# A windowed attention with Fourier mixing: batch 0's scalings on ScalarE, and the whole order of work planned anew

## The chip, the cores and the metric

The kernel runs on one core of a Trainium2 chip. Five engines of the core work side by side, each with its own queue of instructions in a fixed order: TensorE (PE in the profile; its weight loads are PEld), VectorE (DVE), ScalarE (ACT), GpSimd (POOL) and SyncE (SP), which here issues DMAs only. An instruction waits on semaphores for what it needs, and everything behind it in the same queue waits with it. The metric is the device time of one execution in microseconds (us), lower is better; the time of a version is the median of its runs.

## What is computed

Four batches of 8 heads, 768 positions and head size 64. Each position attends to the first 8 positions and to the last 96 ones, with a slope per head. The output x (768 x 512 per batch) goes through a two-dimensional Fourier transform of which the real part is kept, a normalization, and a two-layer network with 2048 hidden values.

```python
scores = scale * np.matmul(q, k.transpose(0, 1, 3, 2)) + bias      # (4, 8, 768, 768)
scores = np.where(is_global | is_local, scores, -1e9)
a = np.exp(scores - np.max(scores, axis=-1, keepdims=True))
attn = np.matmul(a / (np.sum(a, axis=-1, keepdims=True) + 1e-09), v)
x = attn.transpose(0, 2, 1, 3).reshape(B, S, H * D)                # (4, 768, 512)
mixed = np.real(np.fft.fft(np.fft.fft(x, axis=1), axis=2))
u = x + mixed
un = (u - mean(u)) / np.sqrt(var(u) + 1e-06)                       # over the last axis
out = u + np.maximum(un @ w_ch1, 0.0) @ w_ch2
```

## The kernel before

**Stages.** Batch b = 0..3 has four pairs of heads hp = 0..3. For each pair q, k and v are loaded on SP's queue (`load`, token `("ld", 4b+hp, which)`), cast to fp16 (`qk`, `vc`), transposed (`pt` on TensorE for batches 0 and 1, evicted as `qkT`; by DMA for batches 2 and 3), multiplied into scores (`sc`, three groups each), passed through the exponential on ScalarE (`ex`, or `er` and a product on VectorE for batches 2 and 3), and multiplied with v (`av`). `norm` (lines 778 to 785) divides and writes `x`, token `("x", b, hp, jp)` with jp = 0..2. v itself is placed by small matmuls (`pv`) and two evictions, `("v", b, hp, 0)` on VectorE and `("v", b, hp, 1)` on ScalarE.

**The transform.** `fold_s` (lines 813 to 856) adds and subtracts parts of x in four steps f1 to f4, `fold_d` gives the operands `w`, `y_unit` (`py`) and `u_unit` (`pu`) are the two matrix stages, with `mirror` reversing some of y on GpSimd. Batch 0's x is also written to DRAM and read back in another order (`bounce`, tokens `xw` and `xr`) on SP's queue, and batch 1's v loads stand behind that read in the same queue. `u` is the sum, `un` its normalized copy, `ptu` its transpose, `unT` the eviction of that.

**The network.** Each batch gives three chunks, c = 0..11, of 256 positions. `ph(c, j)`, j = 0..7, is one unit of the first layer: 8 matmuls of 256 columns, evicted as `h(c, j)`. `pg(c, t, p)` is a unit of the second layer: 4 matmuls of 512 columns, t = 0, 1, p = 0..3. `ph(c, j)` needs quarter j // 2 of the first weight matrix, w1(j // 2); `pg(c, t, p)` needs quarter p of the second, w2(p). The eight quarters are loaded by eight DMAs on GpSimd's queue (`wload`, lines 1440 to 1457), w1(0) to w2(3) in this order, into memory that first holds batch 1's q and k. The last four chunks use a product scheme with fewer multiplications (`pg_units`, banks `pgA` and `pgD`).

**What sets the order.** Nothing is written in the order in which it runs. Each piece of work is handed to a planner (`Plan`, from line 21) with what it needs, the engines that may do it with a duration for each, and a rank. The planner walks through a model of the engines' clocks and always emits what can start first; `LAND` holds arrival times of some loads, and `BIAS` (lines 142 to 145) adds some microseconds to the start time of single pieces in that comparison, so that they are emitted earlier or later. A PE unit can be chosen from the next 10 of the streams MIX and ATT, and from the head of PH and PG. So a changed duration or preference can move any instruction on any engine. The order that comes out is fixed in the program: what is emitted first on an engine runs first there, and the planner's times play no part on the chip.

**Banks.** Results of TensorE lie in PSUM banks in rings: `xx` has two, `ph` two, `pg` two; C and D exist for the first part only, and the `ph` and `pg` banks take their place, so that the first `ph` unit waits for the last reader of C and D. The planner gives each unit one bank of its ring, and the unit then waits until that bank's eviction is done.

Of the kernel before, what the change touches and what calls it, by code (L numbers as in the profile page):

```python
# [9 lines left out]
FP16 = mybir.dt.float16  # L10
FP32 = mybir.dt.float32
AF = mybir.ActivationFunctionType
ALU = mybir.AluOpType

P = 128
# [7 lines left out]
class Plan:  # L23
# [110 lines left out]
    def slot(self, tag):  # L134
# [4 lines left out]
        return tag  # L139

    LOOK = 10
    BIAS = {(1, 92): -0.3, (3, 34): 0.7, ('h', 7, 7): -3, (2, 58): 3, (3, 69): -1.5, (1, 22): -0.3, ('mk1', 1): -3, (1, 26): -0.7, (2, 46): 0.7,
            ('ex', 0, 1, 1): 0.3, ('h', 2, 0): 1.5, ('h', 2, 6): -0.7, (1, 5): -1.5, ('er', 2): -0.7, (2, 32): -0.7, (3, 45): -1.5, ('er', 0): -0.7,
            (2, 50): -0.7, ('w2t', 0): -1.5, ('ss', 0, 1): -0.7, (3, 66): -1.5, ('unT', 7): 1.5, ('x', 3, 0, 1): -3, ('xb', 14, 0): 0.3,
            (1, 93): -1.5, (2, 35): -3, (3, 22): 0.3, ('ld', 11, 2): 0.7, (2, 36): 0.3, ('y', 1, 2, 3, 'r'): 0.7}
    AHEAD = 0.0

    def run(self, streams):
# [40 lines left out]
def act(n):  # L189
    return 0.06 + n / 1200.0  # L190


def dve(n):
    return 0.085 + n / 960.0


def dve2(n):
    return 0.075 + n / 1920.0
# [7 lines left out]
def kernel(  # L206
# [84 lines left out]
    pl = Plan()  # L291
# [23 lines left out]
    def free(tag, i):  # L315
        i -= NBUF[tag]
        return [("free", tag, i)] if i >= 0 else []

    def buf(tag, i, shape, dtype, users):
        pl.users(("free", tag, i), users)  # L320
        return wk.tile(shape, dtype, tag=f"{tag}_{i % NBUF[tag]}", name=f"{tag}_{i}", bufs=1)
# [186 lines left out]
    def CD(b, ring):  # L508
        if b == 1 and ring in ("C", "D"):
            pl.left[("CD",)][0] += 1  # L510
            return [("CD",)]
        return [("CD",)] if b == 0 else []
# [224 lines left out]
    def av(b, part, jp):  # L737

        half, nh = part[0] // 2, 2 * len(part)
        first = 2 * part[0]  # L740
        needs = [("ex", b, hp, g) for hp in part for g in range(max(jp - 1, 0), jp + 1)]
        needs += VN(b, part)
        if jp:
            needs += [("eg", b, half), ("vG", b, half)]

        def run(start, ring):
            po = bank(ring, f"pav_{b}_{first}_{jp}")
            n = 0
            for jj in range(2):
                j = 2 * jp + jj  # L750
                if jp:
                    nc.tensor.matmul(po[:, jj, 0:65 * nh].rearrange("p (h d) -> p h d", d=65),  # L752
                                     EG[:, (j - 2) * P:(j - 1) * P], vG[b % 2][:, first:first + nh, 0:65],
                                     start=True, stop=False, skip_group_check=True)
                for hh in range(nh):
                    h = first + hh
                    hp, s = h // 2, h % 2
                    ops = [(expst[hp][:, s, j * 256:j * 256 + P], j)]
                    if j:
                        c0 = (j - 1) * 256 + P  # L760
                        ops.append((expst[hp][:, s, c0:c0 + P], j - 1))
                    for a, (lhsT, i) in enumerate(ops):
                        nc.tensor.matmul(po[:, jj, hh * 65:(hh + 1) * 65], lhsT, v16[b % 2][:, i, h, 0:65],  # L763
                                         start=(jp == 0 and a == 0), stop=(a == len(ops) - 1),
                                         skip_group_check=True)
                        n += 1
            e = pl.pe(mm_us(65, n) + (mm_us(65 * nh, 2) if jp else 0), start)
            if jp:
                for _ in part:
                    pl.used(("free", "eg", b), e)  # L770
            if jp == NP - 1:
                for hp in part:
                    pl.tok[("avh", b, hp)] = e
                if part[-1] == HP - 1:
                    pl.tok[("avdone", b)] = e
            pv = po[:, :, 0:65 * nh].rearrange("p j (h d) -> p j h d", d=65)

            def norm():
                if b not in X:
                    X[b] = buf(XT[b][0], XT[b][1], [P, NS, Dm], FP16, 4)  # L780
                rc = wk.tile([P, 2, nh, 1], FP32, tag="rc", name=f"rc_{b}_{first}_{jp}", bufs=2)
                V.reciprocal(rc, pv[:, :, :, 64:65])
                VT(X[b][:, 2 * jp:2 * jp + 2, first * Dh:(first + nh) * Dh].rearrange("p j (h d) -> p j h d", d=Dh),  # L783
                   pv[:, :, :, 0:Dh], rc.to_broadcast([P, 2, nh, Dh]), op=ALU.mult)
            pl.later([("DVE", 0.09 + dve(128 * nh), norm)], free(*XT[b]), e, [("x", b, hp, jp) for hp in part], CD(b, ring),
                     ring=ring, rank=RA(b))
        ATT.append((needs, BANKS(b), run))


    T = {}  # L790
# [22 lines left out]
    def fold_s(b):  # L813
# [3 lines left out]
        for n, (c0, cw) in enumerate(parts):  # L817
# [10 lines left out]
                VT(ab[:, 1], lo, hi, op=ALU.subtract)  # L828

            def f2(c0=c0, cw=cw, n=n, cell=cell):  # L830
                pm = cell["pm"] = buf("ww", IW(b, n), [P, 2, 2, cw], FP16, 1)
                ab = cell["ab"]
                VT(pm[:, 0], ab[:, :, 1], ab[:, :, 2], op=ALU.add)
                VT(pm[:, 1], ab[:, :, 1], ab[:, :, 2], op=ALU.subtract)

            def f3(c0=c0, cw=cw, cell=cell):
                ab, pm, zc = cell["ab"], cell["pm"], T[("z", b)][:, :, c0:c0 + cw]
                VT(zc[:, 0], ab[:, 0, 0], pm[:, 0, 0], op=ALU.add)
                VT(zc[:, 1], ab[:, 1, 0], pm[:, 1, 1], op=ALU.subtract)
                V.tensor_scalar_mul(zc[:, 4], pm[:, 1, 0], c)  # L840
                V.tensor_scalar_mul(zc[:, 5], pm[:, 0, 1], c)

            def f4(c0=c0, cw=cw, cell=cell):
                ab, pm, zc = cell["ab"], cell["pm"], T[("z", b)][:, :, c0:c0 + cw]
                V.scalar_tensor_tensor(zc[:, 2], pm[:, 0, 0], -0.5, ab[:, 0, 0], op0=ALU.mult, op1=ALU.add)
                V.scalar_tensor_tensor(zc[:, 3], pm[:, 1, 1], 0.5, ab[:, 1, 0], op0=ALU.mult, op1=ALU.add)
            last = n == len(parts) - 1
            pl.later([("DVE", 2 * dve2(3 * cw), f1)],
                     [("x", b, hp, jp) for hp in hps for jp in range(NP)] + free("eA", IA(b, n))
                     + (free("zy", 2 * b) if n == 0 else []), 0.0,  # L850
                     [("f1", b, n)], [("free",) + XT[b]] * (2 if len(hps) == HP else 1))
            pl.later([("DVE", 2 * dve2(2 * cw), f2)], [("f1", b, n)] + free("ww", IW(b, n)), 0.0, [("f2", b, n)])
            pl.later([("DVE", 4 * dve2(cw), f3)], [("f2", b, n)], 0.0, [("f3", b, n)])
            pl.later([("DVE", 2 * dve(cw), f4)], [("f3", b, n)], 0.0, [("z", b, n)],
                     [("free", "eA", IA(b, n)), ("free", "ww", IW(b, n))])
        return [("z", b, n) for n in range(len(parts))]

    def IA(b, n):

# [5 lines left out]
    def IW(b, n):  # L865

        return n if b == 0 else 1 + 3 * b + n
# [165 lines left out]
    def u_unit(b, pr):  # L1033
# [4 lines left out]
        def run(start, ring):  # L1038
# [56 lines left out]
                else:  # L1095
                    V.tensor_scalar(cell[0][:, a], UT[c][:, a], SC, m, op0=ALU.mult, op1=ALU.add)  # L1096
            for a in range(2):
                pl.later([("ACT", 0.52, lambda a=a: un("ACT", a)), ("DVE", 0.38, lambda a=a: un("DVE", a))],
                         [("u", c, a)] + free("un", c), 0.0, [("un", c, a)])

            def square(a):
# [473 lines left out]
```

## Time and profile before

| | |
|---|---|
| median of 8 runs | 266.44 us (264.51 to 267.31) |
| the profiled execution | 265.24 us, of which the span of the profile is 263.3 us |
| PE busy | 247.3 us, 94% of the span, 2648 matmuls |
| PEld busy | 181.0 us, 69% |
| DVE busy | 178.6 us, 68%, 366 instructions |
| ACT busy | 140.3 us, 53%, 238 instructions |
| POOL busy | 70.4 us, 27%, 138 instructions |
| mean granted clock | 0.992 |

The span is what the profile shows from the first to the last instruction; 1.94 us of the profiled execution lie around it. Times in the profile are counted from the start of the span. Matmuls are pipelined, so a busy PE can still be waiting for the next operand: a unit's cost is read from the distance between the starts of successive units (a `ph` unit in a full stretch takes 0.87 us, a `pg` unit 0.86 us), not from the busy time. Instructions whose queue entry waits are listed with the idle time in front of them and with what ended it.

### The profile page before, as it was taken

How to read it: one execution, taken by the hardware profiler on the slowest of the kernel's cores; microseconds unless marked ns; L12 is line 12 of the kernel's file. 1: busy time of each engine (PE TensorE's matmuls, PEld its weight loads, DVE VectorE, ACT ScalarE, POOL GpSimd, SP SyncE). 2: the span in 40 equal slices, each digit the busy share in tenths (PEclk: the TensorE clock that was granted, in tenths of full speed). 3: DMA queues.
4: the chain of work that ended last, by engine and by line, in shares of the span. 5: the costliest groups of instructions: out<-in, count | busy, mean ns of one | idle time of the engine just before them, and what ended most of it. 6: DMA issues, size and time to landing. Idle time of an engine off the chain costs nothing.

```text
span 263.3 us, 6439 instructions
## 1 busy us (share of the span) xinstructions
PE 247.3 (94%) x2648; PEld 181.0 (69%) x2648; DVE 178.6 (68%) x366; ACT 140.3 (53%) x238; POOL 70.4 (27%) x138
## 2 busy tenths in 40 slices
PE   8788778899999999899999999999999999999994
PEld 2566456578765786676665565687578968888883
DVE  4458999964389756672579958669997665616173
ACT  1378597777416556793561464993044464353410
POOL 1435358951041145323320352103000411010000
PEclk9799999999999999999999999999999999999999
DMA  7999959999499955965898996403163230402022
GB/s 216 292 293 302 312 141 270 216 212 206 102 211 289 331 126 147 202 166 125 219 172 187 265 219 130 92 12 73 41 159 122 74 88 0 122 0 80 2 80 80
DMA packets 76381, 41.95 MB, mean 159 GB/s; under 512 B 33474, under 2 KB 72514, under 8 KB 76354
## 3 DMA queue, kind: packets, MB, share of 16 engines
q1 hardware_dynamic: 69298, 32.65, 52.2%
q0 software_dynamic: 4224, 4.19, 9.5%
q10 hardware_dynamic: 2832, 4.72, 6.0%
q8 instruction: 20, 0.33, 0.5%
q14 instruction: 7, 0.06, 0.1%
HBM read 31.59 MB, written 9.44 MB: 156 GB/s over the span
## 4 chain that ended last, share of the span: by engine, by line
PE 72%; DVE 15%; ACT 5%; DMA 3%; issue 2%; SPq 1%; POOL 0%; DVEq 0%; ACTq 0%
PE ph L1161 28%; PE pg L1185 20%; PE pgD L1266 5%; PE pav L763 4%; PE pgA L1266 4%; PE py L964 3%; PE pu L1044 3%; ACT er L649 2%; DMA u<-in_v_dram 2%; DVE qkT L581 2%; PE sc L625 2%; PE pav L752 1%; DVE u L1072 1%; DVE un L1096 1%; DVE x L783 1%
## 5 line engine op out<-in xcount | busy, mean ns | idle before, releaser
L1161 PE MATMUL ph<-unT,w 128*128 128x256 f16 x768 | 92.8, 273 | 0.3 <-DVE u L1072 0.3
L1161 PEld LDWEIGHTS <-w 128*128 128x128 f16 x768 | 73.2, 98 | 13.3 <-issue 2.5
L1167 ACT ACTIVATE hT<-ph 128x512 f16<-128x512 f32 x77 | 45.8, 597 | 61.5 <-PE ph L1161 61.4
L1185 PE MATMUL pg<-w,hT 128*128 128x512 f16 x256 | 59.5, 380 | 0.0
L1185 PEld LDWEIGHTS <-hT 128*128 128x128 f16 x256 | 24.1, 98 | 25.0 <-issue 0.6
L649 ACT ACTIVATE er<-sc 128x992 f16<-128x992 f32 (+2 forms) x24 | 21.4, 930 | 7.2 <-PE sc L625 5.4
L652 ACT ACTIVATE ex<-sc 128x992 f16<-128x992 f32 (+2 forms) x24 | 20.7, 931 | 3.4 <-PE sc L628 3.4
L664 DVE TENSOR_TENSOR ex<-er,mk 128x992 f16<-128x992 f16 (+2 forms) x24 | 16.0, 683 | 4.8 <-ACT er L649 4.8
L1012 POOL COPY ww<-zy 128x512 f16<-128x512 f16 x16 | 9.7, 627 | 34.6 <-PE py L964 34.6
L1194 DVE SCALAR_TENSOR_TENSOR u<-pg,sm,u 128x512 f32<-128x512 f32 x16 | 11.9, 746 | 8.9 <-PE pg L1185 8.9
L1168 DVE TENSOR_SCALAR hT<-ph 128x512 f16<-128x512 f32 x19 | 13.1, 687 | 6.9 <-PE ph L1161 6.8
L410 POOL CAST qk<-qs 128x768 f16<-128x768 f32 x12 | 10.1, 848 | 27.3 <-DMA qkT<-qk 13.8
L1110 POOL TENSOR_SCALAR sm<-sm 128x2 f32<-128x2 f32 x12 | 2.5, 211 | 54.3 <-ACT un L1103 52.7
L763 PEld LDWEIGHTS <-ex 128*128 128x128 f16 x352 | 15.1, 97 | 2.8 <-issue 2.1
L763 PE MATMUL pav<-v,ex 128*128 128x65 f16 x352 | 16.4, 193 | 0.2 <-ACT v L486 0.2
L1103 ACT ACTIVATE un<-un 128x512 f16<-128x512 f16 x24 | 15.0, 625 | 0.6 <-PE ptu L1133 0.6
L1063 DVE SCALAR_TENSOR_TENSOR u<-pu,xr 128x512 f32<-128x512 f32 x18 | 11.7, 687 | 5.2 <-PE pu L1044 5.2
L1284 DVE SCALAR_TENSOR_TENSOR u<-pgD,sm,u 128x512 f32<-128x512 f32 (+1 forms) x9 | 6.2, 691 | 11.2 <-PE pgD L1266 11.0
L1266 PEld LDWEIGHTS <-hT 128*128 128x128 f16 x128 | 12.5, 98 | 1.8 <-issue 0.4
L783 DVE TENSOR_TENSOR x<-pav,rc 128x512 f16<-128x512 f32 (+1 forms) x21 | 12.9, 615 | 0.7
L539 POOL COPY kG<-qkT 64x8 f16<-64x8 f16 x32 | 7.8, 245 | 16.7 <-DVE qkT L581 13.6
L496 POOL CAST v<-qs 128x768 f16<-128x768 f32 x8 | 7.4, 923 | 18.2 <-DMA qs<-in_v_dram 18.2
(122 smaller groups left out, 386.6 us busy)
## 6 DMA issues: line engine op xcount, KB each, us to landing
out_dram<-u SPq DMA_DIRECT2D x23, 256.0 KB, 2.2
w<-in_moe_w_ch_dram POOLq DMA_DIRECT2D x8, 512.0 KB, 19.2
qs<-in_q_dram SPq DMA_DIRECT2D x9, 384.0 KB, 3.9
qs<-in_k_dram SPq DMA_DIRECT2D x9, 384.0 KB, 5.4
qs<-in_v_dram SPq DMA_DIRECT2D x16, 192.0 KB, 4.5
xr<-xd ACTq DMA_DIRECT2D x3, 768.0 KB, 5.0
u<-in_v_dram SPq DMA_DIRECT2D x5, 384.0 KB, 7.4
w<-in_q_dram SPq DMA_DIRECT2D x4, 384.0 KB, 6.3
```

Source lines behind the costliest of these rows:

```text
L649: A(mine(), cut(pa), AF.Exp, 0.0, 0.125)
L652: A(cut(expst[hp][:, :, g * 512:g * 512 + (384 if g == 2 else 512)]), cut(pa), AF.Exp, 0.0, 0.125)
L664: VT(o, mine(), m, op=ALU.mult)
L763: nc.tensor.matmul(po[:, jj, hh * 65:(hh + 1) * 65], lhsT, v16[b % 2][:, i, h, 0:65], start=(jp == 0 and a == 0), stop=(a == len(ops) - 1) ...
L783: VT(X[b][:, 2 * jp:2 * jp + 2, first * Dh:(first + nh) * Dh].rearrange("p j (h d) -> p j h d", d=Dh), pv[:, :, :, 0:Dh], rc.to_broadcast( ...
L1103: A(x, x, AF.Square, accum_out=MV[c][:, a, 2:3])
L1161: nc.tensor.matmul(ph[:, a * CH:(a + 1) * CH].rearrange("p (x m) -> p x m", x=2), W1[0][:, d, jb * P:(jb + 1) * P], UNT[c][:, :, d, :], st ...
L1167: pl.later([("ACT", act(512), lambda: A(dst, ph, AF.Relu)), ("DVE", dve(512), lambda: V.tensor_scalar_max(dst, ph, 0.0))], [], e, [("h", c ...
L1168: ("DVE", dve(512), lambda: V.tensor_scalar_max(dst, ph, 0.0))],
L1185: nc.tensor.matmul(pg, HT[c][:, jb, t * P:(t + 1) * P], W2[0][:, jb, :], start=(jb == 0), stop=(jb == NJ - 1))
L1194: V.scalar_tensor_tensor(UT[c][:, t, :], pg, MV[c][:, t, 3:4], UT[c][:, t, :], op0=ALU.mult, op1=ALU.add)
L1266: nc.tensor.matmul(o, lhs(j), rhs(j), start=(first and j == 0), stop=(j == NK - 1), skip_group_check=True)
```

## The change

One pair of instructions goes to another engine: for batch 0, the products of two sums with a constant (`zc[:, 4]` and `zc[:, 5]`, 256 columns, two parts, so four instructions) move from VectorE, step f3, to ScalarE, as a step of its own, f5. The buffer `ww` that both read has then two users. The durations that the planner takes for some VectorE work are changed: `norm` (0.09 to 0.2), f1 and f2 of the first part of batch 0 (plus 0.9 and 0.6), `un` of the first two chunks (0.38 to 1.3). The list `BIAS` is another one, with 125 entries where there were 30. No computation is added or left out.

```diff
-    BIAS = {(1, 92): -0.3, (3, 34): 0.7, ('h', 7, 7): -3, (2, 58): 3, (3, 69): -1.5, (1, 22): -0.3, ('mk1', 1): -3, (1, 26): -0.7, (2, 46): 0.7,
...
+    BIAS = {(2, 58): 3, (3, 69): 0.3, (1, 26): -1.5, (2, 46): 0.7, ('ex', 0, 1, 1): 0.3, (2, 32): -0.7, (2, 50): -0.7, ('ss', 0, 1): -0.7,
...
-            pl.later([("DVE", 0.09 + dve(128 * nh), norm)], free(*XT[b]), e, [("x", b, hp, jp) for hp in part], CD(b, ring),
+            pl.later([("DVE", 0.2 + dve(128 * nh), norm)], free(*XT[b]), e, [("x", b, hp, jp) for hp in part], CD(b, ring),
...
-                pm = cell["pm"] = buf("ww", IW(b, n), [P, 2, 2, cw], FP16, 1)
+                pm = cell["pm"] = buf("ww", IW(b, n), [P, 2, 2, cw], FP16, 1 if b else 2)
...
+            def f5(c0=c0, cw=cw, cell=cell):
+                pm, zc = cell["pm"], T[("z", b)][:, :, c0:c0 + cw]
+                for o, i in ((zc[:, 4], pm[:, 1, 0]), (zc[:, 5], pm[:, 0, 1])):
+                    if b:
+                        V.tensor_scalar_mul(o, i, c)
+                    else:
+                        A(o, i, AF.Copy, 0.0, c)
...
-                V.tensor_scalar_mul(zc[:, 4], pm[:, 1, 0], c)
-                V.tensor_scalar_mul(zc[:, 5], pm[:, 0, 1], c)
+                if b:
+                    f5(c0, cw, cell)
...
-            pl.later([("DVE", 2 * dve2(3 * cw), f1)],
+            pl.later([("DVE", 2 * dve2(3 * cw) + 0.9 * (b + n == 0), f1)],
...
-            pl.later([("DVE", 2 * dve2(2 * cw), f2)], [("f1", b, n)] + free("ww", IW(b, n)), 0.0, [("f2", b, n)])
-            pl.later([("DVE", 4 * dve2(cw), f3)], [("f2", b, n)], 0.0, [("f3", b, n)])
+            pl.later([("DVE", 2 * dve2(2 * cw) + 0.6 * (b + n == 0), f2)], [("f1", b, n)] + free("ww", IW(b, n)), 0.0, [("f2", b, n)])
+            pl.later([("DVE", (4 if b else 2) * dve2(cw), f3)], [("f2", b, n)], 0.0, [("f3", b, n)])
+            if b == 0:
+                pl.later([("ACT", 2 * act(cw), f5)], [("f2", b, n)], 0.0, [("f5", b, n)], [("free", "ww", IW(b, n))], rank=0)
...
-        return [("z", b, n) for n in range(len(parts))]
+        return [("z", b, n) for n in range(len(parts))] + [("f5", b, n) for n in range(len(parts)) if b == 0]
...
-                pl.later([("ACT", 0.52, lambda a=a: un("ACT", a)), ("DVE", 0.38, lambda a=a: un("DVE", a))],
+                pl.later([("ACT", 0.52, lambda a=a: un("ACT", a)), ("DVE", 1.3 if c < 2 else 0.38, lambda a=a: un("DVE", a))],
```

The order that the planner makes of this differs on every engine. For the first 70 us it does this (names as above; the identity is the constant that the transposes and the placing of v use):

| engine | before | changed |
|---|---|---|
| SP | q, k of pair 0, identity, masks, v | identity, q, k of pair 0, masks, v; batch 1's v in the order of pairs 2, 0, 3, 1 instead of 0, 1, 2, 3 |
| DVE to ACT | | casts of pair 0's q and k; `qkT` of pairs 0, 2 and 7; f5, two parts; `un(0, 0)`, `un(1, 1)` |
| ACT to DVE | | `qkT` of pair 6; cast of q of pair 3; one of two `vG` evictions of batch 0; `un(2, 1)` |
| ACT and POOL | casts of q: pair 4 on ACT, pairs 5 and 7 on POOL | pair 4 on POOL, pairs 5 and 7 on ACT |
| POOL | the eight weight DMAs with kG copies and `mirror`'s copies between them | the eight weight DMAs with one kG copy and one mask copy between them, `mirror`'s copies behind them |
| PE, first chunk | ptu1, ph(0, 0), ph(0, 1), ptu2, ph(0, 2), pv1.1, ph(0, 3), av, ph(0, 4) to ph(0, 7), ph(1, 0), pv1.2, ph(1, 1), ph(1, 2), pg(0, 0, 0), ph(1, 3), ph(1, 4), pg(0, 0, 1) | ph(0, 0) to ph(0, 2), ptu2, ph(0, 3) to ph(0, 7), pv1.1, pg(0, 0, 0), av, pg(0, 0, 1), ptu1, pv1.2, pv1.3, ph(1, 0), pvg1, av, ph(1, 1) |

## The prediction

> **What bounds the kernel now.** First the page's head, then busy time by stretch.
>
> ```profile
> span 263.3 us, 6439 instructions
> PE 247.3 (94%) x2648; PEld 181.0 (69%) x2648; DVE 178.6 (68%) x366; ACT 140.3 (53%) x238; POOL 70.4 (27%) x138
> ```
> ```profile
> 25.00:53.40 28.40, 21.74 (x371) 15.18 (x371) 27.50 (x63) 21.43 (x34) 18.60 (x31) 1.00 1.00 238
> 53.40:67.00 13.60, 13.40 (x147) 11.09 (x148) 6.59 (x12) 8.64 (x22) 4.99 (x9) 1.00 1.23 207
> 180.00:250.00 70.00, 70.00 (x625) 56.51 (x622) 45.39 (x86) 28.75 (x55) 6.92 (x15) 1.00 0.24 69
> ```
>
> The columns are the stretch, then busy us of PE, PEld, DVE, ACT, POOL, the granted clock, DMA share, GB/s. From 25 to 53.4 us VectorE is busy 27.50 of 28.40 us; afterwards PE is. Third, the chain of waits: VectorE to 53.25, then the first `ph` unit.
>
> ```profile
> 36.51 0.76 DVE zy L840
> 37.28 0.77 DVE zy L841
> ...
> 53.25 0.14 issue
> 53.39 0.71 PE ph L1161 x5
> ```
>
> Fourth, the timeline of PE, from which I took the distance between starts of successive units. After 53.39 nearly every unit follows at its usual pace; the true stalls behind it are 0.38 us at 56.8, then 1.02 (at 107.4), 0.24, 0.27, 0.34, 0.13 and 0.17, 2.17 us together after 70 us. So a later stage cannot give back much: an earlier end must come from an earlier start of the network or from those 2.17 us.
>
> Fifth, the DMA view of single GpSimd issues, for the weights (column after the size: us from issue to landing), and SP's waits, where SP holds the next loads until the last quarter has landed, at 69.65.
>
> ```profile
> w<-in_moe_w_ch_dram POOLq DMA_DIRECT2D x1, 512.0 KB, 20.1
> ```
> ```profile
> SPq L1459 <- DMA w<-in_moe_w_ch_dram: 27.5, 1, 27.5
> ```
>
> The first line is the issue at 44.49, w2(1): it landed at 44.49 + 20.1 = 64.6. In the same way w1(0) to w2(0) landed at 47.9, 52.8, 56.4, 59.5 and 62.1. pg(0, 0, 1), which needs w2(1), started only 3.0 us after its landing:
>
> ```profile
> 64.97 1.03 PE L1185 MATMUL pg<-w,hT 128*128 128x512 f16 x4
> 65.83 1.91 PE L1161 MATMUL ph<-unT,w 128*128 128x256 f16 x16
> 67.58 1.03 PE L1185 MATMUL pg<-w,hT 128*128 128x512 f16 x4
> ```
>
> **The change, part by part.** *The scalings.* Four instructions leave VectorE: 0.14 + 0.14 us of its chain in the first part, 0.76 + 0.77 in the second, where GpSimd was casting beside them (36.2 to 38.0):
>
> ```profile
> 28.89 0.21 DVE L840 TENSOR_SCALAR zy<-ww 128x256 f16<-128x256 f16 x1
> 36.44 0.84 DVE L840 TENSOR_SCALAR zy<-ww 128x256 f16<-128x256 f16 x1
> ```
>
> That is 1.81 us. On ScalarE no row has 256 columns from SBUF; one column took 0.20 (L1084), 384 took 0.49 and 512 took 0.60, so 0.20 to 0.49 each; I take 0.38 on the line through the last two, 0.76 a part. Work behind it: in the first part ex of pair 3, then eg, wait for it; the second has f3, f4 of VectorE as cover (about 1.1 us).
>
> The Trainium skill, "ScalarE: Activation LUTs", Rules for kernel authors, says to keep multiplications on VectorE because it is up to three times faster per element. The first row agrees with that (0.14 against 0.38), the second does not (0.76); by the rule alone the move would cost ScalarE 4 x 0.24 = 1 us and win nothing.
>
> *The other exchanges.* Leaving VectorE after 23.5 us: qkT of pair 7 (0.87 in the chain), un(0, 0) (0.67), un(1, 1) (0.86). Joining it: qkT of pair 6 (0.95 by L581), one vG eviction (0.41). VectorE's sum to the first `ph` is 1.81 + 0.87 + 0.67 + 0.86 - 0.95 - 0.41 = 2.85 us shorter, so at best ph(0, 0) starts at 50.5. ScalarE gains 1.52 + 2 x 0.71 and two casts of 0.84 and loses one of 0.84 and 0.37: 21.43 + 3.4 = 24.8 of some 26 us; it fits, tightly. GpSimd's mirror copies now stand behind the last weight DMA, which costs pu0.1 and pu0.2 up to 0.5 us. So 50.5 to 51.5.
>
> *The identity ahead of q and k.* It delays the two loads by its 64 KB (384 KB land every 1.35 us, so 0.2 us) and removes a wait of 0.84 us for it at 6.40. The first exponentials still stand behind the same v eviction on ScalarE, whose v landed at 8.1. Nothing by 13.5 us, plus or minus 0.5.
>
> *The weights.* They come down a saturated path: from w2(0) on one quarter lands every 2.5 us, and DMA share is 1.23. What can move them is the start of that traffic. It begins with the read-back `xr`, issued at 37.27, 3.76 us after the last x of batch 0 (33.51), and with w1(0)'s issue at 38.04. In the new order qkT of pair 2 is on ScalarE behind a v eviction (it ends at 20.8, against 20.2), but av of the first pairs comes ahead of the next scores; f1 starts some 4 us earlier, and runs beside GpSimd's casts as before. Then ScalarE's ex, cast, f5, ex, ex, eg end at 29.2 to 29.5, and VectorE does qkT of pair 4 to 29.85 and four pieces of x at 0.55 each: 32.1, so `xr` is 1.4 us earlier. w1(0) waits for kG after qkT of pair 6 on VectorE, at 36.3 to 37.0, 1.0 to 1.7 earlier. I take 1.4; bounds 0 (ScalarE late, below) and 2.5. w2(0) then lands at 60.7, w2(1) at 63.2.
>
> *Batch 1's v loads* landed at 43.1, 47.4, 53.0 and 58.3 (issues of L402), each 1.4 earlier now; in the order 2, 0, 3, 1 pair 0's comes at 46.0, before pv1.0 at 50, and pair 1's at 56.9, before pv1.1 at 58 or later: nothing.
>
> *TensorE's order, where this is paid.* Before, 13 `ph` units stood ahead of pg(0, 0, 1); now 8, and ptu1 stands behind it, on which ph(1, 0) and all its followers depend. From ph(0, 0) at 50.5 the eight units, ptu2 and pv1.1 end by 58.3 without waits; w1(3) at 58.1 and w2(0) at 60.7 hold PE up already, and pg(0, 0, 1) cannot start before 63.2. From there: pg 0.86, ptu1 0.45, eviction of unT 0.75 with its hops, pv1.3 0.22, so ph(1, 0) at 65.5. The evictions of pv1.3 are on VectorE and then on ScalarE, behind a square (0.49 + 0.8 + 0.49 and hops): av of pairs 2, 3 waits for them until 2.0 us after the start of ph(1, 0), 67.5, and ph(1, 1) starts at 67.9. Before, the same set of units was finished when ph(1, 6) began at 70.45, with five more `ph` units done, so it corresponds to 70.45 - 5 x 0.873 = 66.1. Loss here: 1.8 us. The 2.85 us that VectorE gains only lengthen PE's wait.
>
> *Later.* Gone: the 1.02 us at 107.4, where ptu5 stood just behind VectorE's un (it now stands some 10 us later in PE's order); most of the 0.34 + 0.13 at the end (four more units between the last h and its sums). New: ph(2, 1) and ph(2, 2) follow each other on the same bank, so the second waits for an eviction (0.60 by L1167, and hops): 0.73. py1.0 waits for w of batch 1: 0.35. Around 165 to 178 ScalarE's squares stand ahead of er: 0.5 where 0.27 was. Five more changes from other units to score units, 0.1 each. Of the 2.17 us remain 0.41; with 0.73 + 0.35 + 0.5 + 0.5 that is 2.5 and a little less if some are covered; I take 2.1, no change. Bounds 0.6 (the new ones covered) and 3.5.
>
> **Sum.** +1.8 - 0.1 = +1.7 on the profiled execution's own 265.24 us: 266.9. That execution is 1.2 us below the median of the runs shown (266.44), so for a median I expect 268.1.
>
> **The rivals.** *VectorE's relief arrives (R1).* If the weights land 3 us earlier or more, the walk above without weight waits gives ph(1, 1) at 65.3, 0.8 ahead; with 1.4 of the later stalls gone it is 2.2 under: 264.2. It decides from a landing of w2(1) at 61.5. For it: the sixth of the page's 40 slices, 33 to 39 us, moved 141 GB/s where the ones around it moved 312 and 270, so there is room for an earlier start. Against: the same bytes must still pass before w2(1). *Given back later (R2).* The weights set the pace, but the new later waits are all covered and the old ones gone: 1.8 - 1.3 = +0.5, 266.9 as a median; no change. *ScalarE becomes the bound (R3), slower.* From 18 to 30 us it carries qkT of pair 2 (1.45 against 0.95 on VectorE) between v's eviction and the exponentials; if eg then ends after 30.8 instead of 29.4, x is no earlier than before, the weights neither, and the loss at ph(1, 1) is 1.8 + 1.4 = 3.2: 269.6. For it: 24.8 of 26 us busy. Against: ScalarE waited 2.75 us at 32.6. *The change doesn't do what it says:* that VectorE gets no shorter, because other copies run beside GpSimd's casts instead. Then ph(0, 0) is at 53.4 as before, which w2(0) and w2(1) hide: the loss at ph(1, 1) stays at 1.8, so this is no case of its own.
>
> **How the numbers follow.** Weights set the pace, as summed: 0.40 (its own range 266.9 to 269.3: weights 0.4 us either way, later waits by half of their bounds). R1 0.20, R2 0.27, R3 0.13. Within 0.5%, 1.3 us, is about what a measurement of this kernel can tell from no change. Faster: most of R1, 0.20. Same: R2, and the low edge of the first: 0.28. Slower: the rest, 0.52. Range: down to R1's 264.2 less nothing, up to R3's 269.6 and a little more: 264.4 to 270.0, which leaves about 2 in 10 out.
>
> **What would show it.** Right: ph(0, 0) at 50.5 to 51.5; w2(1) landing at 62.9 to 63.6 and pg(0, 0, 1) starting with it, PE idle some 4 us between ph(0, 0) and ph(1, 1); ph(1, 1) near 67.9; ph(2, 2) behind an eviction. Wrong: a landing of w2(1) under 61.5, ph(1, 1) under 66.5, or ptu1 done before ph(0, 7).

## The result, and the profile after

The changed kernel takes 270.2 us (median of 11 runs, 269.41 to 272.68), the kernel before 265.65 us (32 runs). The ratio is 1.0177, with a 95% interval of 1.015 to 1.0205: slower by 4.6 us, where 268.1 was predicted with a range up to 270.0, a loss of 1.7 us on the 266.44 of the eight runs known then. The direction was right and the size too small. Ratios are of the executions within 1.5% of the fastest of their kernel; in the runs below that leaves out at most 2, but 4 of 10 in the first and 7 of 12 in the last, which are less sure for it.

The page's head, with the span and the busy time of each engine:

```profile
span 266.4 us, 6448 instructions
PE 246.2 (92%) x2648; PEld 179.8 (67%) x2648; DVE 175.0 (66%) x356; ACT 150.0 (56%) x251; POOL 72.6 (27%) x135
```

ScalarE has 9.7 us more, VectorE 3.6 us less, as the change meant, and TensorE is not busier. The loss is therefore idle time of TensorE. Busy time by stretch (columns as before: the stretch, PE, PEld, DVE, ACT, POOL, granted clock, DMA share, GB/s) says where:

```profile
25.00:53.40 28.40, 21.86 (x373) 15.95 (x373) 24.42 (x57) 25.00 (x42) 16.16 (x29) 1.00 1.02 243
53.40:67.00 13.60, 10.99 (x131) 8.26 (x130) 4.96 (x10) 7.18 (x17) 4.43 (x7) 1.00 1.21 202
```

In the first stretch VectorE falls from 27.50 to 24.42 us and is no longer full. In the second TensorE falls from 13.40 of 13.60 us to 10.99. The timeline of TensorE in that stretch, with the idle time in brackets ahead of a row and what ended it:

```profile
60.73 0.36 PE L481 MATMUL pvp<-v,ident 64*64 64x128 f16 x12
61.48 1.02 PE L1209 MATMUL pg<-w,hT 128*128 128x512 f16 x4 [0.39 <-DMA w<-in_moe_w_ch_dram]
62.34 0.58 PE L777 MATMUL pav<-v,ex 128*128 128x65 f16 x12
64.01 1.02 PE L1209 MATMUL pg<-w,hT 128*128 128x512 f16 x4 [1.08 <-DMA w<-in_moe_w_ch_dram]
64.87 0.61 PE L1157 MATMUL ptu<-ident,un 128*128 128x128 f16 x8
65.41 0.36 PE L481 MATMUL pvp<-v,ident 64*64 64x128 f16 x12
66.26 0.36 PE L481 MATMUL pvp<-v,ident 64*64 64x128 f16 x12 [0.49 <-DVE unT L1167]
66.56 1.05 PE L1185 MATMUL ph<-unT,w 128*128 128x256 f16 x8
```

Both waits for a quarter of the weights are there: pg(0, 0, 0) starts at the landing of w2(0) at 61.44, pg(0, 0, 1) at that of w2(1) at 63.97, and only then come ptu1, its eviction unT and ph(1, 0). ph(1, 1) starts at 68.31.

One caution on this page. Of twelve executions of the changed kernel it is the one with the shortest span: the others have 267.4 to 270.6 us, at a granted clock of 0.985 to 1.0 (this one 1.0; the one before had 0.992, and 0.93 in its first 25 us). Around its span lie 3.0 us, in the others 1.9 to 2.1. So its 3.1 us of longer span understate the loss. Two more profiles of the same order, taken below, have spans of 267.4 and 267.1.

### The profile page after: what moved, and what is told of

The parts are those of the page before. It is cut to its first block, busy times and chain, and to the rows that moved or that the text cites. A ratio compares the mean times of both kernels' runs of the same rounds, so it can differ in the third digit from the quotient of the medians.

```text
span 266.4 us, 6448 instructions
## 1 busy us (share of the span) xinstructions
PE 246.2 (92%) x2648; PEld 179.8 (67%) x2648; DVE 175.0 (66%) x356; ACT 150.0 (56%) x251; POOL 72.6 (27%) x135
## 4 chain that ended last, share of the span: by engine, by line
PE 68%; DMA 11%; SPq 7%; DVE 6%; ACT 4%; issue 2%; POOL 2%; POOLq 0%; ACTq 0%; DVEq 0%
PE ph L1185 27%; PE pg L1209 17%; DMA w<-in_moe_w_ch_dram 8%; SPq L416 6%; PE pgD L1290 5%; PE pgA L1290 4%; PE pav L777 3%; PE pu L1068 3%; PE py L988 3%; DMA w<-in_q_dram 3%; PE sc L639 2%; POOL w L1469 1%; PE pav L766 1%; SPq L1395 1%; ACT er L663 1%
## 5 line engine op out<-in xcount | busy, mean ns | idle before, releaser
L1191 ACT ACTIVATE hT<-ph 128x512 f16<-128x512 f32 x80 | 47.5, 597 | 58.4 <-PE ph L1185 56.9
L678 DVE TENSOR_TENSOR ex<-er,mk 128x992 f16<-128x992 f16 (+2 forms) x24 | 15.3, 647 | 16.8 <-ACT er L663 16.7
L666 ACT ACTIVATE ex<-sc 128x768 f16<-128x768 f32 (+2 forms) x24 | 21.0, 922 | 2.8 <-PE sc L642 2.6
L1134 POOL TENSOR_SCALAR sm<-sm 128x2 f32<-128x2 f32 x12 | 4.0, 334 | 64.4 <-ACT un L1127 64.2
L1118 ACT ACTIVATE un<-u,sm 128x512 f16<-128x512 f32 x12 | 8.5, 717 | 8.7 <-DVE sm L1091 8.5
L1192 DVE TENSOR_SCALAR hT<-ph 128x512 f16<-128x512 f32 x16 | 11.0, 686 | 3.0 <-PE ph L1185 2.2
L553 POOL COPY kG<-qkT 64x8 f16<-64x8 f16 x32 | 8.8, 280 | 12.3 <-DVE qkT L595 9.0
```

What stands on the lines that cost most here:

```text
L666: A(cut(expst[hp][:, :, g * 512:g * 512 + (384 if g == 2 else 512)]), cut(pa), AF.Exp, 0.0, 0.125)
L678: VT(o, mine(), m, op=ALU.mult)
L1191: pl.later([("ACT", act(512), lambda: A(dst, ph, AF.Relu)), ("DVE", dve(512), lambda: V.tensor_scalar_max(dst, ph, 0.0))], [], e, [("h", c ...
```

## The experiments

In all of them the planner is left out: the sequence in which it emitted its 993 pieces (991 before), with each piece's engine and bank, is written out as a list, and an experiment moves entries of that list. Everything not named stays where it was, which a changed preference could not promise. The diffs show the moves (what evicts or squares the result of a moved unit moves with it). Ratios are to the kernel before on the same chip, with 95% intervals.

Three theories are named in what was expected. W: the quarters of the weights set TensorE's pace, because pg(0, 0, 1) now stands ahead of ptu1 and of all of ph(1, .). E: the work that VectorE and ScalarE exchanged delays what TensorE waits for. L: the later waits alone make the loss.

### The stage of the weights, put into the kernel before

```diff
  # the list of the kernel before
  PE: ... ph0.7
+ PE: pg0.0.0, pg0.0.1, ptu1, pv1.2
  PE: ph1.0
...
- ptu1 ahead of ph0.0; pv1.2, ph1.1, ph1.2 ahead of pg0.0.0; ph1.3, ph1.4 ahead of pg0.0.1
```

> The kernel before with its own order kept, but with pg(0, 0, 0) and pg(0, 0, 1) moved up behind ph(0, 7), and ptu1 with ph(1, 0) behind them, as the changed kernel has them; scalings on VectorE. Theory W, if this order alone is enough: ph(0, 7) ends at 61.95, pg(0, 0, 0) runs from 62.1, pg(0, 0, 1) waits from 63.0 to the landing of w2(1) at 64.6, and ptu1 with its eviction comes then: 1.6 to 2.6 us slower than before, 267.3 to 268.3 against 265.65 (ratio 1.006 to 1.010). Theory E or L: the order in this stage costs nothing by itself, 265.2 to 266.1 (ratio 0.998 to 1.002).

Measured: 1.0099 (1.0039 to 1.016), 2.6 us. The timeline of TensorE in this run:

```profile
61.59 1.03 PE L1275 MATMUL pg<-w,hT 128*128 128x512 f16 x4
63.69 1.02 PE L1275 MATMUL pg<-w,hT 128*128 128x512 f16 x4 [1.07 <-DMA w<-in_moe_w_ch_dram]
64.55 0.61 PE L1223 MATMUL ptu<-ident,un 128*128 128x128 f16 x8
65.09 0.36 PE L557 MATMUL pvp<-v,ident 64*64 64x128 f16 x12
65.95 1.26 PE L1251 MATMUL ph<-unT,w 128*128 128x256 f16 x10 [0.49 <-DVE unT L1233]
```

The same picture as in the changed kernel, made in a kernel that has nothing else of the change. The waits (1.23 us above the usual distance, then 0.69 for the eviction of unT and 0.2 behind it) add up to 2.1 us, and all of it is still there at the last unit, which starts at 260.79, 258.67 before. Theory W is enough for this much; E and L can't be the whole.

### The wait alone, taken out of the changed kernel

```diff
- W2[0][:, jb, :]
+ W2[0][:, jb - 4 * (c + t == 0 and part == 1), :]
```

> The changed kernel's own order kept word for word; in the one unit pg(0, 0, 1) the matmuls read the rows of w2(0) in place of those of w2(1), so this unit's part of the sum is another, and it no longer waits for w2(1); all loads stay. Theory W: TensorE's wait before pg(0, 0, 1), 1.30 us by the trace, goes; w2(0) at 61.4 still holds pg(0, 0, 0). pg(0, 0, 1) at 62.7 instead of 64.0, ph(1, 1) at 67.0 instead of 68.3, time 268.9 (268.6 to 269.3). Theory E: what stands behind it (ptu1's eviction, the evictions of v, av) takes over at once, gain under 0.4: 269.8 to 270.5.

Measured: 269.04 us, 1.0116 (1.0011 to 1.022). The median is the one that W expected, but the interval holds the changed kernel's 1.0177 too, so the time alone shows no gain. The trace does, up to this place: pg(0, 0, 1) started at 62.52 and ph(1, 1) at 66.83, 1.5 us earlier than in the changed kernel's first profile, although ph(0, 0) came 0.6 us later (52.84). But in this profile 1.7 us came back at 129 us, at a place that has nothing to do with weights; it comes again below.

### Putting ph units back ahead of the wait: first a miss

```diff
  # the changed list
+ PE: ptu1 behind ph0.3; unT_1 behind it
+ PE: ph1.0, ph1.1, ph1.2, ph1.3, with their evictions, ahead of pg0.0.0
```

> The changed kernel's own order kept word for word (every engine's list, the banks), but with ptu1 and four units of ph(1, .) moved ahead of pg(0, 0, 0) in TensorE's list, and their evictions with them, as in the kernel before; nothing else moves. Theory W (the quarters of the weights set TensorE's pace between 57 and 66 us, because pg(0, 0, 1) now stands ahead of ptu1 and of all ph(1, .)): the 3.5 us of ph units fill the wait for w2(0) and w2(1), pg(0, 0, 1) starts some 1 to 2 us after the landing of w2(1) and no longer with it, and the time falls by 1.8 to 2.4 us, from 270.2 to 267.8 to 268.4 (ratio to before 1.008 to 1.010). Theory E (the shares that VectorE and ScalarE exchanged delay what TensorE waits for): no gain, 269.7 to 270.7. Theory L (the later waits alone, py1.0, ph2.2 and the like): no gain at the end, since what is won at 66 us is lost by 90: 269.7 to 270.7.

Measured: 1.0222 (1.0127 to 1.0317), not faster than the changed kernel. The wait for w2(1) did go, but the list of waits on TensorE from 60 to 80 us shows what the move had done to the other engines:

```profile
PE pvp L557 <- POOL v L541: 1.1, 1, 1.1
PE pav L842 <- ACT vG L776: 0.7, 1, 0.7
PE ph L1261 <- DVE hT L1268: 0.7, 1, 0.7
PE pvg L765 <- DVE v L575: 0.4, 1, 0.4
```

The columns are what waited for what: us in total, times, longest. With four ph units gone from behind the v units, nothing lay between a v unit and the evictions that the next one needs. A wait was exchanged for a chain of short ones. Some 5 us were lost from 68 to 78 us: 2.7 of them are idle time in such waits, and from 73 to 78 us the granted clock was 0.66 in this profile (1.00 ahead of it and behind), where a ph unit took 1.51 us. The profile is of the longest of the four executions, 273.46 us, the others took 271.15 to 271.62; what the chain costs in the median isn't shown.

### The whole stage as before, in the changed kernel

```diff
  # the changed list, between ph0.0 and pg0.0.2: the order and engines of the list before
- SP: ld_6_2, ld_4_2, ld_7_2, ld_5_2
+ SP: ld_4_2, ld_5_2, ld_6_2, ld_7_2
```

Beside it ran the changed kernel itself:

> The changed kernel once more, with its order written out word for word in place of the scheduler, so that the other three have a control on the same chip. All theories: 1.015 to 1.020 of the kernel before. Its trace should again show pg(0, 0, 1) starting with the landing of w2(1), and the profile of this execution should tell whether the 3.0 us around the span of the first profiled execution (2.0 to 2.1 in other executions) come again: I expect 2.0 to 2.1 and a span of 267.4 to 269.

> The changed kernel's own order up to ph(0, 0) and from pg(0, 0, 2) on; the stage between them, some 52 to 77 us, arranged as in the kernel before (TensorE's units, the evictions' engines, ptu1 ahead of ph(0, 0), thirteen ph units ahead of pg(0, 0, 1)), with batch 1's four v loads in the order that this needs. Theory W: ph(0, 0) at 52.7 (0.45 for ptu1 ahead of it), pg(0, 0, 0) at 64.3 and pg(0, 0, 1) at 66.9, both well behind their quarters (61.4, 64.0), so nothing waits, and pg(0, 0, 2) starts 2.3 to 2.9 us earlier than the changed kernel's 77.3; the time falls by as much, 1.007 to 1.010 of before. Theory E: below 0.7 us of gain, 1.014 or more. Theory L: the gain of 2.3 to 2.9 at pg(0, 0, 2) is there but is lost again by 130 us; 1.014 or more.

Measured: the changed kernel 1.016 (1.0134 to 1.0187), with the stage as before 1.0106 (1.0077 to 1.0136). Some 1.4 us are won, less than the 2.3 to 2.9 expected, and 2.8 us of loss remain. pg(0, 0, 0) and pg(0, 0, 1) started at 64.60 and 67.21, with no wait, and at pg(0, 0, 2), where both have done the same units, TensorE was 3.3 us ahead of the changed kernel beside it, the control (74.67 against 78.00; 0.9 of it from an earlier start). Then it lost 0.49 ahead of pg(1, 0, 0), where the control lost nothing, and 0.94 and 0.80 around py1.0 (0.29 and 0.67 in the control): 2.0 us were left at the end. What TensorE wins at 66 us makes it arrive at work of batch 1 that is not ready.

### The later waits

```diff
  # the changed list
- DVE: h_1_6 (behind y_1_2_0)
+ ACT: h_1_6 (behind ph1.7)
+ PE: pg1.0.3 directly behind pg1.0.2;  ph2.0 to ph2.3 on banks 0, 1, 0, 1
```

> The changed kernel's own order with only this moved: the eviction of ph(1, 6) on ScalarE behind that of ph(1, 5), and not on VectorE some 14 us later, so that both banks of the ph units are free again and ph(2, 0) to ph(2, 3) alternate between them; and pg(1, 0, 3) directly behind pg(1, 0, 2), ahead of py1.0. Theory L: the waits of 0.85 us (ph(2, 2) behind an eviction on its own bank) and most of 0.66 us (py1.0 behind w of batch 1) go and stay gone: 1.2 to 1.5 us faster than the changed kernel, 1.012 to 1.013 of before. Theory W: the same, since the terms add; the stage around 57 to 68 us is unchanged, with pg(0, 0, 1) at w2(1)'s landing. If what is won is given back to a later load or eviction: 1.016 to 1.019.

Measured: 1.0125 (1.0089 to 1.016) against 1.016. In the profile both waits are gone (the last pg units ahead of pgl2 start at 127.06, 1.2 us earlier than in the control), and 1.46 us are lost at 129, ahead of pgl2: the same place as in the run without the wait for w2(1).

```diff
  # stage_plus: both repairs.  stage_plus_v: both, and DVE: f5_0_n behind f3_0_n
```

> Both repairs in the changed kernel: its stage from ph(0, 0) to pg(0, 0, 2) arranged as in the kernel before (as in the run that did this alone), and the eviction of ph(1, 6) on ScalarE behind that of ph(1, 5), with pg(1, 0, 3) behind pg(1, 0, 2). The rest of the changed order and the scalings on ScalarE stay. Theory W and L together (the loss is those two places): the first repair is worth 2.0 to 2.8 us, the second up to 1.5, of a loss of about 4.3: 1.000 to 1.005 of before. If a later load takes over, as in the run with the second repair alone (1.46 us of wait before pgl2 at 129 us): 1.006 to 1.010. Theory E (something spread over all engines): not under 1.009.

> Both repairs in the changed kernel, as in the run before with both (1.0073), and the four scalings back on VectorE, so that nothing is left of the change but its first 52 us and its order from 77 us on. If the scalings on ScalarE cost about 1 us in this order (1.010 to 1.012 against 1.016 to 1.018 in the two runs so far): 1.002 to 1.005. If they cost nothing: 1.006 to 1.009.

Measured: 1.0073 (1.0038 to 1.0107) and 1.0116 (1.0072 to 1.016). The scalings on VectorE do not help here; the two intervals overlap. Neither is at 1.000, so with both known places repaired something remains. The waits on TensorE from 66 to 140 us in the first of the two show where:

```profile
PE pg L1285 <- DVE u L1294: 1.0, 1, 1.0
PE py L1064 <- DVE ww L1023: 0.5, 1, 0.5
PE py L1064 <- DVE zy L1081: 0.4, 1, 0.4
```
All three are VectorE's work of batch 1, in the later order. Is it that order by itself, or the front? This puts the later order behind the front of the kernel before:

```diff
  # the list before up to pg0.0.2, then the changed list with the repair of the later waits
```

> The kernel before, scalings on VectorE, its own order up to pg(0, 0, 2) (77 us), and from there the changed kernel's order with the same two repairs as in the run with both (the eviction of ph(1, 6) early, pg(1, 0, 3) behind pg(1, 0, 2)). What is left of the loss there, 0.7%, 1.9 us, is either in the order from 77 us on or in the first 52 us. If it is later: 1.005 to 1.009 of before, with waits at pg(1, 0, 0), py1.0 or pgl2 in the trace. If it is in the front: 0.996 to 1.002 (the changed kernel has 1.02 us less of a stall at 107 and some 0.3 more at 170).

Measured: 1.0112 (1.0069 to 1.0155), 3.0 us. So the order from 77 us on costs by itself, scalings, front and weights as before. The waits on TensorE from 75 to 135 us:

```profile
PE pgl L800 <- ACT er L739: 1.5, 1, 1.5
PE py L1054 <- DVE zy L1071: 0.9, 1, 0.9
PE py L1054 <- DVE ww L1014: 0.5, 1, 0.5
PE pg L1275 <- DVE u L1284: 0.3, 1, 0.3
```

and ScalarE at the first of them:

```profile
128.89 0.84 ACT L496 ACTIVATE qk<-qs 128x768 f16<-128x768 f32 x1 [1.74 <-DMA qs<-in_q_dram]
129.64 0.95 ACT L739 ACTIVATE er<-sc 128x960 f16<-128x960 f32 x1
```

Three are VectorE's, the same as in the run with both repairs: w and y of batch 1 and the addition ahead of pg(1, 0, 0) come too late for a TensorE that is on time. The fourth is a load of q (issued at 121.73) that took some 7 us; ScalarE's cast of it stands ahead of an exponential for which TensorE waits. In the first profile of the changed kernel that load took 3.8 us. The wait shows in 3 of 13 profiles with this later order and in no clear relation to how early TensorE comes, so I count it as scatter that this order lets through.

### The scalings

In the changed order, back on VectorE:

```diff
- ACT: f5_0_0, f5_0_1
+ DVE: f5_0_0 behind f3_0_0, f5_0_1 behind f3_0_1
```

> The changed kernel's own order kept, with the four scalings of batch 0 back on VectorE, just behind the other two operations of f3, and gone from ScalarE's list. VectorE's chain to ph(0, 0) is longer again by 0.3 to 1.8 us (0.14 to 0.77 each, by whether GpSimd casts beside them), ScalarE's list shorter by 1.42. Theory W: ph(0, 0) moves from 52.3 to 52.6 to 54.0, but w2(1) lands at 64.0 as before and TensorE waits for it anyway: no difference that can be measured, 269.8 to 270.8. Theory E1 (ScalarE's added work is what costs): faster by 1 us or more, under 269.2. Theory E2 (VectorE still sets the end, so its relief was worth its length): slower by 1 us or more, over 271.2.

> The changed kernel's own order with the scalings back on VectorE, once more, because its first profile was a disturbed one. Its fast times so far, 268.7 to 269.7 against some 270.2 of the changed kernel, speak for a cost on ScalarE of some 0.5 to 1 us. If that holds: 1.011 to 1.014 of before, eg of pairs 2 and 3 ends at least 0.5 us earlier behind the start of f1 than in the changed kernel (7.96 us there, from 21.45 to 29.41), and VectorE waits less for qkT of pair 5's input (0.99 us there). If it doesn't hold (theory W: hidden behind w2(1)): 1.015 to 1.019 and pg(0, 0, 1) at the landing of w2(1) as before.

> The changed kernel, as the control of the next run on the same chip: 1.014 to 1.020 of before.

> The changed kernel's order with the scalings back on VectorE, on the same chip as the changed kernel itself. If the scalings on ScalarE cost: 1.009 to 1.013 of before, at least 0.8 us under the run before this one. If the lower times of the two runs so far were chance: 1.014 to 1.018, within 0.4 us of the run before this one.

Measured: 1.0118 (1.0014 to 1.0221), 1.0101 (1.0048 to 1.0154), and on one chip side by side 1.0156 (1.0108 to 1.0204) against 1.0146 (1.0093 to 1.0199) of the changed kernel. The first two runs looked like a gain of 1 us; the direct comparison shows none, and the profile of the second shows eg no earlier behind f1 (8.24 us, 7.96 in the changed kernel). Whether the scalings cost anything in this order is not shown to better than 0.5%; they are at most a small part of the loss.

In the order before, on ScalarE:

```diff
  # the list before
+ ACT: f5_0_0 behind eg_0_1, f5_0_1 behind ex_1_0_2   (and out of VectorE's f3)
```

> One part of the change alone: the kernel before with its own order kept, and the four scalings on ScalarE, the first two behind eg of the pairs 2 and 3, the other two behind ex(1, 0, 2). VectorE's chain to ph(0, 0) is shorter by 1.81 us, by the durations of the profile before. If VectorE sets the end there and nothing takes its place: ph(0, 0) at 51.6 to 52.2 instead of 53.4, pg(0, 0, 0) and pg(0, 0, 1) at 63.3 to 63.8 and 65.9 to 66.4, still behind their quarters (62.1, 64.6), and the time falls by 1.2 to 1.8 us, 0.993 to 0.996 of before. If VectorE only waits longer (for qkT's input, GpSimd's copies or ScalarE's exponentials): ph(0, 0) within 0.5 us of 53.4, 0.998 to 1.002. If the 1.4 us that ScalarE gets delay its exponentials and with them TensorE: slower, 1.003 or more.

> The kernel before with only the scalings on ScalarE, once more, as the control of the next run and to see whether 0.995 stands: 0.993 to 0.997. Its first profile showed no relief of VectorE up to ph(0, 0) (28.14 us from the start of f1 to ph(0, 0), 28.08 before): the two operations behind the scalings, z, took 2.00 us beside GpSimd's two casts, 0.75 before. I expect the same here: z of the second part over 1.6 us, f1 to ph(0, 0) 27.6 to 28.4, and a missing stall of 1.0 us near 107.

Measured: 0.9951 (0.9931 to 0.9971) and 0.9965 (0.993 to 1.0001). Faster, but not where it was priced. VectorE behind f3 of the second part, and GpSimd beside it, in the first of the two:

```profile
36.81 0.28 DVE L936 TENSOR_TENSOR zy<-eA,ww 128x256 f16<-128x256 f16 x1
37.02 0.28 DVE L937 TENSOR_TENSOR zy<-eA,ww 128x256 f16<-128x256 f16 x1
37.22 1.04 DVE L943 SCALAR_TENSOR_TENSOR zy<-ww,eA 128x256 f16<-128x256 f16 x1
38.18 1.04 DVE L944 SCALAR_TENSOR_TENSOR zy<-ww,eA 128x256 f16<-128x256 f16 x1
```
```profile
37.01 1.94 POOL L500 CAST qk<-w 128x768 f16<-128x768 f32 x2
```

The two scalings are gone from between the second and the third line. Before, they stood beside the casts, and z behind them:

```profile
37.20 0.85 DVE L841 TENSOR_SCALAR zy<-ww 128x256 f16<-128x256 f16 x1
37.96 0.41 DVE L845 SCALAR_TENSOR_TENSOR zy<-ww,eA 128x256 f16<-128x256 f16 x1
```
```profile
36.22 1.74 POOL L410 CAST qk<-w 128x768 f16<-128x768 f32 x2
```

They took 0.84 and 0.85, and the two operations of z 0.41 each. Now z itself stands beside GpSimd's two casts and takes 1.04 each. What looked like the price of the scalings was the price of whatever VectorE does from SBUF to SBUF beside these casts: 1.26 of the 1.81 us went to z. From f1 of the first part to ph(0, 0) pass 28.14 us in both runs, 28.08 before: no relief at all. Most of the rest went to the two `un` of chunk 0, first before, then in this run:

```profile
47.60 1.75 DVE L1096 TENSOR_SCALAR un<-u,sm 128x512 f16<-128x512 f32 x2
```
```profile
48.27 2.19 DVE L1196 TENSOR_SCALAR un<-u,sm 128x512 f16<-128x512 f32 x2
```

Why they are 0.44 us longer no run shows. The Trainium skill, "SBUF — State Buffer", Who interferes with whom, states the rule: a VectorE instruction with two SBUF inputs, or one in a two-port mode, and a GpSimd instruction that reads SBUF exclude each other, and the second waits until the first is done. The lines agree: each operation of z ends some 0.3 us behind a cast.

A check of that reading, with the operation that reads PSUM put beside the cast instead:

```diff
  # the run above, and
- ACT: qkT_6      POOL: qk_7_0
+ DVE: qkT_6 between f3_0_1 and z_0_1      ACT: qk_7_0
```

> The run before this one, with two more moves: qkT of pair 6 on VectorE (which reads PSUM) between f3 and z of the second part, and the cast of q of pair 7 on ScalarE in its place. If GpSimd's casts are what stretches VectorE's operations from SBUF to SBUF, and qkT isn't stretched (0.95 us with or without casts in the profile before): z of the second part takes 0.75 us again, VectorE's chain is 0.3 us shorter in all, ScalarE's 0.6 shorter, and the time 0.2 to 0.8 us under that of the run with the scalings alone: 0.991 to 0.995 of before. If the stretch of z had another cause: z stays near 2.0, VectorE's chain is 0.95 longer and the time 0.996 to 1.000.

```profile
38.78 0.96 DVE L671 COPY qkT<-pt 128x1536 f16<-128x1536 f16 x1
39.65 0.41 DVE L943 SCALAR_TENSOR_TENSOR zy<-ww,eA 128x256 f16<-128x256 f16 x1
39.98 0.42 DVE L944 SCALAR_TENSOR_TENSOR zy<-ww,eA 128x256 f16<-128x256 f16 x1
```

GpSimd's cast ran from 38.57 to 39.54. z is back at 0.41, and qkT beside the cast takes 0.96, as alone. The time is 0.9974 (0.9937 to 1.0011), not under that of the control (0.9965): the reading held, the gain expected from it did not come. VectorE waited 0.70 us for the transpose ahead of another qkT instead (f1 to ph(0, 0): 28.12 us), and TensorE waits 0.9 us for ScalarE's er near 107, as in the kernel before.

Where then does the gain of the scalings alone come from? It comes behind ph(0, 0): from there to the last unit pass 205.28 us before, 204.43 and 203.95 in the two runs. Both of their profiles lack the stall of 1.02 us at 107. VectorE there in the kernel before, and then in a run that only moves a cast on GpSimd:

```diff
  # the list before
- POOL: v_2_3, qk_11_0
+ POOL: qk_11_0, v_2_3      (and the load into v_2_3's buffer behind it)
```

> The kernel before, its own order, scalings on VectorE; one move on GpSimd: the cast of v of pair 11's predecessor (v of batch 2, fourth pair), which runs from 105.88 to 106.86 beside VectorE's second un of the unit 5 (106.09 to 107.14, 1.05 us), goes behind the cast of q of pair 11, whose load lands at 106.57; the load that reuses its buffer goes behind it. If the gain of the scalings alone (0.9951 and 0.9965 of before) is no more than the stall of 1.02 us at 107, which was missing in both of its profiles: un takes 0.48 us, the stall at 107 is under 0.3 us, and the time falls by 0.7 to 1.1 us, 0.995 to 0.998. If the stall isn't that cast's doing: it stays at 1.0 and the time at 0.999 to 1.002.

> Both: the scalings on ScalarE in the order of the kernel before, and the cast moved as in the run before this one. If the two gains are the same gain: no better than either alone, 0.995 to 0.998. If the scalings are worth something by themselves up to ph(0, 0) or to f1 of batch 0: 0.991 to 0.994.

```profile
105.69 1.45 DVE L1096 TENSOR_SCALAR un<-u,sm 128x512 f16<-128x512 f32 x2 [0.47 <-DVE sm L1067]
107.06 1.29 DVE L664 TENSOR_TENSOR ex<-er,mk 128x992 f16<-128x992 f16 x1
```
```profile
106.80 0.88 DVE L1186 TENSOR_SCALAR un<-u,sm 128x512 f16<-128x512 f32 x2 [0.48 <-DVE sm L1157]
107.59 0.67 DVE L754 TENSOR_TENSOR ex<-er,mk 128x992 f16<-128x992 f16 x1
```

The first fence is the kernel before, where two casts run beside these lines (105.88 to 107.82), the second the run with the move, where they run from 108.10 to 109.71. Without scalings on ScalarE the move gives 0.9951 (0.9914 to 0.9987); with both it is 0.9964 (0.9907 to 1.002), no better as far as so wide an interval tells. From ph(0, 0) to the last unit these two take 204.12 and 204.43 us; the run with the two more moves, which has the scalings on ScalarE and the stall, takes 205.85. So the gain goes with the stall, wherever the scalings are: the scalings alone shift VectorE past it, and do not shorten its chain. The scalings alone and the moved cast alone are some 0.4% faster than the kernel before, and so than both kernels of this case.

## Why the prediction was right and wrong, by its steps

**The bound and the mechanism** were right. TensorE waits for w2(0) and w2(1), because pg(0, 0, 1) stands ahead of ptu1 and all of ph(1, .); made by itself in the kernel before, this order costs 2.1 us in the trace and 2.6 in the time, where the step said 1.8. What failed are sizes. Two of the terms below that were wrong reach the time: the weights, with 2.2 to 2.9 us lost in the stage instead of 1.8, and the later waits, with 0.9 to 1.3 us more lost instead of 0.1 won.

**"The scalings. ... That is 1.81 us"** failed. The relief of VectorE's chain to ph(0, 0) was nothing in the order before. 1.53 of the 1.81 were the two scalings beside GpSimd's casts, and the next operations paid for these casts (1.26 us), and un for 0.44 more. The other price, 0.76 us a part on ScalarE, was right: 0.71 and 0.72 measured. The rule of the Trainium skill weighed there ("ScalarE: Activation LUTs", Rules for kernel authors) gave the right outcome for this chain, no win, for another reason than the one that the runs show: 0.36 us a scaling on ScalarE is more than 0.21 on VectorE alone and less than 0.84 beside a cast.

**"at best ph(0, 0) starts at 50.5 ... So 50.5 to 51.5"** failed: 52.25, and 53.34 and 52.44 in the two further profiles. VectorE's sum was shorter, but it waited. In the first profile:

```profile
33.32 0.96 DVE L595 COPY qkT<-pt 128x1536 f16<-128x1536 f16 x1 [1.00 <-PE sc L642]
...
35.32 0.43 DVE L847 TENSOR_TENSOR ww<-eA 128x512 f16<-128x512 f16 x1
35.66 1.05 DVE L848 TENSOR_TENSOR ww<-eA 128x512 f16<-128x512 f16 x1
```

It waits 1.00 us for the transpose of pair 5, which stands behind score units on TensorE, and the second operation of f2 meets a cast (35.33 to 36.43) and takes 1.05 instead of 0.41. The step summed instructions and gave no price to what VectorE itself waits for.

**"The weights ... I take 1.4"** failed for the same reason. x of batch 0 was done at 32.33, as worked out (32.1), and eg ended at 29.41, so the rival that had ScalarE late (eg behind 30.8, x no earlier) is not what happened, and that its 269.6 lies near the result is chance. But these 1.6 us stand between x and kG of pair 6, and w1(0) was issued at 38.26 instead of 36.3 to 37.0 (38.04 before). The read-back `xr` went out at 36.60, 0.67 us earlier than before and not 1.4. w2(1) landed at 63.97, and at 64.70 and 64.32 in the other profiles, against 64.58 before: 0.6 us earlier at most, not 1.4.

**The stage's sum, 1.8 us**, then follows with the later landing: ph(1, 1) at 68.31 (67.9 predicted), 69.05 and 68.66, against 66.1 for the same work before: 2.2, 2.9 and 2.6 us.

**"Later ... I take 2.1, no change"** is the other step that failed and reaches the time. Three of its terms were there: py1.0 waits 0.66 (0.35 predicted), ph(2, 2) 0.85 (0.73), and the stall at 107 is gone. The first two in the first profile, by the distance between starts:

```profile
87.00 0.83 PE L988 MATMUL py<-t,ww 128*128 128x256 f16 x6 [0.48 <-DVE ww L948]
89.38 1.03 PE L1185 MATMUL ph<-unT,w 128*128 128x256 f16 x8 [0.69 <-ACT hT L1191]
```
But the last unit starts 3.1 us later than before in the first profile (261.76 against 258.67) and 4.1 and 3.9 in the others, so 0.9 to 1.3 us more are lost after ph(1, 1), not 0.1 won. And the run with the later order alone says more: by itself it costs 3.0 us. In the changed kernel part of that hides behind the wait for the weights, because a TensorE that is late finds VectorE's work of batch 1 done: the wait ahead of pg(1, 0, 0), 0.3 to 1.0 us, is in all four profiles of the later order in which the stage of the weights is as before, and in none of the nine others. The two alone, 2.6 and 3.0, add up to more than the 4.6 of both (by the medians; the intervals would allow a plain sum), and putting the stage of the weights back gives 1.4, less than the 2.6 that it costs alone. The 3.0 is with the two later waits repaired already, so that repair is no measure of it. I had looked for new waits only in the order as it would run late, and took the covered ones for free.

**From the profiled execution to the median** I added 1.2 us for both kernels alike. The profile after is of an execution 0.8 us under its median. Besides, the median of the kernel before is 265.65 with 32 runs, 266.44 with the eight known then: 0.8 of the 4.6 us are this.

Shown by experiment: the cost of the stage's order, the cost of the later order, GpSimd's casts as the price of VectorE's operations, and that the scalings alone shorten nothing up to ph(0, 0) and gain only where the stall is missing. Only argued: the share of each lost term in the changed kernel, and that the two losses cover each other, since the intervals are about 0.4% wide either way. Open: how much of the 1.0073 and 1.0116 with both places repaired is the three waits of batch 1, why the later order has them, and whether the scalings cost anything in the changed order.

## What to carry to other kernels

Before pricing an instruction that is moved away, look at what ran beside it on the other engines: if its length is a wait for a shared resource, the next instruction can inherit it. Two losses in series on one engine can cover each other, so test a new order's stages one at a time in the old kernel as well as by repairing them in the new one. And when TensorE's order brings a unit closer to the landing of its data, write down what stands behind it in the queue: here it was a 0.45 us transpose on which all following units hung.

## What was not expected of the hardware

The same VectorE operation (256 columns, two SBUF inputs) takes 0.41 us alone and 1.04 us beside a GpSimd cast, while a copy from PSUM takes 0.96 us in both cases. Whether two such instructions meet can hang on some tenths of a microsecond, and here it decides 1 us at 107.

One and the same load of 384 KB, issued at the same point of the program, landed after 3.8 us in one profile and some 7 in another. And one program's span varied by 4.2 us over twelve executions (266.4 to 270.6), so that a single profile, here the shortest, can hide a third of a loss.
